# Loading k and v of batch 0 over SyncE's queue as 32-bit words in a fused attention and gated feed-forward kernel

## The chip, the cores and the metric

The kernel runs on one core of one Trainium2 chip. The metric is device time in microseconds, the median of the runs. The core has five engines with a queue each, worked through in order: TensorE (PE in the profile; PEld is its weight load), VectorE (DVE), ScalarE (ACT), GpSimd (POOL) and SyncE (SP). SyncE and GpSimd issue DMAs, which 16 DMA engines carry out. SBUF is the working memory with 128 partitions, PSUM the memory that TensorE writes.

## The reference

Eight batches of attention with keys and values averaged over groups of 8 rows, followed by a gated convolution feed-forward layer. Inputs and the output are 32-bit floats.

```python
# q, k, v: (8 batches, 8 heads, 576 rows, 64)
k_p = k.reshape(B, H, 72, 8, D).mean(axis=3)
v_p = v.reshape(B, H, 72, 8, D).mean(axis=3)
scores = (1/sqrt(D)) * q @ k_p.T
attn = softmax(scores)
x = (attn @ v_p), heads side by side            # (8, 576, 512)
h = maximum(x @ w_in, 0)                        # (8, 576, 1024)
c = sum over 3 taps of conv_w[tap] * h shifted by tap - 1 rows
out = (h * sigmoid(c)) @ w_out                  # (8, 576, 512)
```

## The kernel before

All arithmetic but the sums in PSUM is on 16-bit floats (bf16). Inputs are 32-bit in memory; GpSimd's DMAs convert them while they load (`nc.gpsimd.dma_start`), so every load of q, k, v and the weights stands in GpSimd's queue. SyncE's queue holds the convolution weights' load (L566), the stores of the output (L1106, L1116), and for batches 5 to 7 transposing DMAs (qT at L777, xT at L881).

Each batch goes through the same steps. **Loads**: `load_k` (L493 for 512 rows, L497 for the last 64), `load_v` (L526 main part, L533 and L538 for the tail), `load_q` (L456, L450). k_b, v_b and q_b have two buffers each, batch b uses number b % 2. **k**: VectorE adds 8 neighbours in three steps (L683, L691, L704), TensorE transposes the sums (L717, L718), and two copies spread them into kz (L724). **q**: a regrouping copy q<-q_b (L464, batches 0 to 4), transposes on TensorE (L794), copies to qT (L803). **v**: the same pooling (L683, L691, L754) and two masked products into vblk (L764, L759). **Attention**: scores on TensorE (L826, L828), exp on ScalarE (L834), five row tiles of attention times v (L851, L855; called av), division by the sum on VectorE (rr L864, xx L868), and the transpose of xx to xT (TensorE L891, L889 with copies L897; a DMA from batch 5 on). **Feed-forward**: x times w_in (L911 for batch 0, L934 for the others), the clipped result hT (L918, L940), convolution either as products on VectorE and ScalarE (cv: L982, L980, L989, L999) or on TensorE (L1057), the gate tg on ScalarE (L1007, L1064), its rescaling where the gate is a tanh (L1035), the product gT (L1045), and for each pair of batches the output projection with w_out (L1088), its copy to osb (L1111, L1101) and the store.

The order of all instructions is made when the program is built. `Planner.add` records every step with its engine, an assumed cost, what it reads and writes, and a priority; `Planner.order` then takes the steps one after the other by the earliest start that its costs give and, among equals, by the number in `PARAMS["prio"]`. Steps that may run on ScalarE or VectorE run on ScalarE if `PARAMS["act"]` names them. The program is emitted in that order, and each engine's queue keeps it; semaphores are added only where data, a buffer or one of the eight semaphore lanes of a DMA queue demand it. The planned order is all that carries over: an assumed cost is no wait. Where the planner finds TensorE waiting in the first 60 us, it emits filler matmuls on a tile of zeros (L418, from `warm`), which stand in TensorE's queue like any other instruction.

Before the change, GpSimd's queue starts with: the last 8 rows of q of batch 0 (L456), k of batch 0 (L493, L497), the identity matrix, one tail of v, the first 64 rows of q (L456), then the two halves of v (L526) with the other tails (L533) and the mask's instructions (L617, L621) between them, k of batch 1, and w_in. The staging tiles that the change uses are parts of gT, which batch 0 and 1 fill only from 30 us on:

```python
def early(i, lo, hi):
    return gT[i].rearrange("p f s -> p (f s)")[:, lo:hi].bitcast(FP32)
ks = early(1, 0, NT * 1024).rearrange("p (t e) -> p t e", t=NT)
ws = early(0, 0, NT * 1024).rearrange("p (t e) -> p t e", t=NT)
```

Of the kernel before, what the change touches and what calls it, by code (L numbers as in the profile page):

```python
# [14 lines left out]

PARAMS = {
    "prio": (
        "9 18 2 13 23 17 24 21 48 19 31 16 33 27 53 30 41 43 47 59 61 10 44 40 34 39 28 25 "
        "37 71 38 36 29 62 32 46 22 15 3 11 6 54 8 12 5 1 64 7 0 26 42 14 35 49 45 20 "
        "4 78 81 51 55 91 95 173 209 50 57 60 63 58 56 66 52 82 83 98 101 65 74 75 80 88 72 73 "  # L20
        "89 76 92 110 93 94 84 87 69 79 77 68 70 90 108 99 102 105 111 114 122 97 129 113 117 86 96 100 "
        "106 109 104 115 120 125 130 116 119 123 132 131 103 67 112 121 144 127 137 133 139 147 179 172 182 187 189 203 "
        "186 193 107 190 197 207 218 213 192 200 216 219 210 215 221 222 194 224 229 261 238 242 248 232 240 246 251 255 "
        "236 228 241 250 253 243 244 247 257 279 245 252 256 263 267 118 124 148 151 142 145 161 166 178 176 167 171 162 "
        "181 184 196 198 135 136 140 143 128 134 138 141 153 152 159 160 146 149 157 165 168 183 175 169 170 180 156 174 "
        "163 188 201 205 204 211 214 225 150 155 154 158 164 202 185 85 177 208 195 235 227 271 277 284 287 295 312 331 "
        "329 342 345 346 357 355 371 374 191 126 233 199 206 212 217 220 226 231 230 234 254 223 260 270 237 239 262 265 "
        "276 283 269 282 264 258 327 333 325 339 274 266 353 358 368 365 377 383 391 375 367 381 379 394 376 378 384 414 "
        "417 397 402 401 437 446 413 416 422 439 444 272 281 285 290 321 317 286 298 291 299 302 324 338 307 316 296 304 "
        "343 348 320 310 335 334 336 356 361 289 303 301 314 337 341 311 306 315 319 322 349 352 280 288 268 273 308 293 "  # L30
        "305 278 330 318 350 354 359 363 386 393 387 403 410 429 463 449 454 464 500 512 515 249 259 292 275 294 300 313 "
        "370 372 382 362 373 396 407 389 405 399 392 297 326 332 328 366 360 427 441 415 420 436 440 411 419 425 431 450 "
        "451 455 471 474 461 468 434 530 535 487 504 501 534 541 489 483 502 508 518 494 511 509 537 542 481 490 503 510 "
        "496 523 514 536 528 533 552 546 568 572 478 495 516 524 525 529 498 548 538 549 554 562 600 611 531 540 467 472 "
        "621 628 475 479 484 485 497 638 639 539 551 521 527 555 560 581 545 570 563 595 598 647 650 656 666 592 609 698 "
        "683 694 696 710 715 309 323 344 340 347 351 380 388 395 400 412 409 424 426 418 423 421 438 459 574 582 430 565 "
        "390 398 404 432 406 466 469 442 448 452 457 473 476 480 488 547 544 532 571 578 585 590 593 602 608 588 594 597 "
        "612 618 596 603 607 620 625 601 610 616 587 624 553 566 550 558 567 604 619 586 627 631 652 645 657 651 606 613 "
        "564 573 617 583 630 589 644 659 671 653 699 700 579 584 614 626 605 623 637 629 633 648 660 663 686 690 556 576 "
        "575 580 661 655 640 641 670 679 691 681 695 705 720 736 741 689 721 734 756 768 750 773 766 783 802 369 364 428 "  # L40
        "408 443 433 435 447 453 458 658 692 677 664 684 513 591 561 445 519 456 462 465 505 493 729 733 711 726 707 714 "
        "727 735 731 739 747 757 767 777 764 769 771 791 780 786 788 793 784 781 796 804 787 799 795 808 632 636 615 634 "
        "675 669 673 662 687 693 706 704 723 728 643 649 635 642 682 708 665 742 722 748 754 759 770 790 646 688 654 674 "
        "701 697 703 719 730 737 738 746 755 761 667 678 672 680 716 713 743 724 744 758 765 763 749 782 792 732 801 809 "
        "816 812 822 842 850 854 460 482 557 543 477 470 486 492 506 507 718 709 668 725 702 491 385 499 526 599 517 520 "
        "522 622 685 762 775 800 797 776 779 774 785 745 751 806 813 798 814 815 818 819 824 817 820 827 832 849 847 925 "
        "857 831 858 856 867 825 828 823 821 837 829 839 834 843 845 860 851 855 871 875 877 866 865 886 878 888 874 889 "
        "897 900 907 915 917 852 853 859 862 864 869 881 872 873 880 879 890 893 899 833 835 895 892 861 884 848 882 894 "
        "904 921 913 923 927 933 943 946 941 952 950 965 966 955 962 985 996 997 559 569 577 778 789 794 753 752 740 760 "
        "772 676 712 717 807 803 830 836 810 838 840 844 805 811 841 846 863 868 826 870 901 905 909 912 914 920 922 928 "  # L50
        "940 931 937 939 930 936 945 949 885 887 876 883 934 911 938 898 953 959 964 960 973 976 916 926 924 951 919 956 "
        "957 961 947 980 983 978 992 993 908 918 891 906 929 932 948 942 935 944 958 954 968 967 902 910 896 903 972 971 "
        "975 969 986 984 1009 990 1010 1011 1013 1019 1026 1034 1030 1036 1046 1041 1047 1020 1001 1015 998 988 1027 991 1017 1007 1023 1025 "
        "1028 1029 1035 1039 1016 1021 970 977 1031 1040 987 1002 989 999 1008 1043 1044 979 994 995 1000 1022 1024 1003 1004 1006 1014 1012 "
        "1018 1033 974 981 963 982 1005 1037 1032 1038 1072 1042 1051 1045 1049 1048 1054 1056 1052 1050 1055 1057 1053 1058 1061 1066 1073 1059 "
        "1062 1065 1060 1063 1067 1069 1068 1064 1070 1071 "
    ),
    "off": [(0, 2, 3, 6, 7), (0, 3, 4, 6, 7), (0, 1, 2, 3, 5, 6, 7), (0, 1, 2, 3, 4, 5, 6, 7), (0, 1, 2, 3, 4, 5, 6, 7), (0, 1, 2, 3, 4, 5, 6, 7), (0, 1, 2, 3, 4, 5, 6, 7), (0, 1, 3, 5, 7)],
    "seq": "",
    "sw": [0, 1, 0, 0, 1, 0, 0, 1],  # L60
    "fuse": [0, 0, 0, 0],
    "act": (
        "dw1.0 dw1.1 dw2.0 dw2.1 dw2.2 dw4.0 dw4.1 dw5.0 dw5.1 dw5.2 dw6.0 dw6.2 "
        "kz.0.0 qg.0.0 qTe.0.3 xte.0.0 xte.0.1 xte.0.2 xte.0.3 xte.0.4 kz.1.0 kz.1.1 qTe.1.2 xte.1.0 "
        "xte.1.1 xte.1.2 xte.1.3 xte.1.4 cp2.0.3 cp0.0.7 cp2.0.6 oe.0.0 oe.0.1 oe.0.2 kz.2.0 kz.2.1 "
        "qg.2.0 qTe.2.2 xte.2.0 xte.2.3 cp2.1.0 cp0.1.3 cp2.1.3 cp0.1.7 oe.0.4 oe.0.5 oe.0.7 oe.0.8 "
        "kz.3.1 qg.3.0 qg.3.4 qTe.3.0 qTe.3.1 qTe.3.2 xte.3.1 xte.3.4 cp2.2.0 cp0.2.3 cp0.2.5 oe.1.0 "
        "oe.1.1 oe.1.2 kz.4.0 kz.4.1 qTe.4.0 qTe.4.1 qTe.4.2 xte.4.0 xte.4.1 xte.4.2 xte.4.4 cp2.3.1 "
        "cp0.3.2 cp2.3.2 cp0.3.4 cp2.3.6 oe.1.4 oe.1.6 oe.1.7 oe.1.8 cp0.4.2 cp0.4.3 cp2.4.4 oe.2.0 "
        "oe.2.1 oe.2.2 kz.6.0 kz.6.1 cp2.5.3 cp2.5.4 cp0.5.6 cp0.6.0 cp2.6.0 cp2.6.2 cp2.6.3 cp0.6.4 "  # L70
        "cp2.6.4 cp2.6.5 cp2.6.6 oe.3.0 oe.3.1 oe.3.2 cp0.7.0 cp2.7.1 cp2.7.5 oe.3.4 oe.3.5 oe.3.8.0 "
        "oe.3.8.1 "
    ),
    "shift": {},
    "tail": [291.3594, -207.6026, 217.4942, 142.1234, 247.0674],
# [27 lines left out]
    "xw": 1,  # L103
    "qd": [0, 0, 0, 0, 0, 0, 0, 0],
    "vp": [0, 0, 0, 0, 0, 0, 0, 0],
    "kh": 0,
    "sp": [0, 0, 0, 0],
}

# [8 lines left out]
class Planner:  # L118
# [60 lines left out]
    def order(self):  # L179
# [23 lines left out]
        while avail:  # L203
# [68 lines left out]
            if o.dma is not None:  # L272
                n, each = o.dma
                if e == "SP" and s < 20.0 and o.lat is not None:
                    o.done = s + d + 2.03
                elif e == "SP" and s < 20.0:
                    hring = max(hring, s + d + 0.5, 3.9, max(ring)) + n * each
                    ring = [max(z, hring) for z in ring]
                    o.done = hring + self.DMA_LAT
                elif e == "SP":  # L280
                    late = max(ring) > s + d + 1.0
                    hring = max(hring, s + d + (4.5 if late else 0.5)) + n * each + (1.4 if late else 0.0)
                    for z in range(4):
                        ring[z] += n * each + 0.2 if late else 0.0
                    o.done = hring + (self.DMA_LAT if o.lat is None else o.lat)
                else:
                    w = (3,) if o.width == 1 else range(o.width)
                    for z in w:
                        ring[z] = max(ring[z], s + d + self.DMA_GAP)
                        ring[z] += n * each * (1.2 if ring[z] < 12.0 else 1.0 if ring[z] < 28.0 else 1.08)  # L290
                    x = max(ring)
                    land = x + self.DMA_LAT + (0.0 if x < 28.0 else 1.0)
                    o.done = x + (self.DMA_LAT if o.lat is None else o.lat) + (0.0 if x < 28.0 else 1.0)
            else:
                o.done = s + d + (self.LAT[e] if o.lat is None else o.lat) + self.SEM
            if e == "POOL" and o.dma is not None:
# [21 lines left out]
def kernel(  # L318
# [77 lines left out]
    pl = Planner()  # L396
# [442 lines left out]
    def attn_av(b, t, pr):  # L839
# [39 lines left out]
        if PARAMS["tx"][b]:  # L879
            def fn(e):  # L880
                nc.sync.dma_start(out=xT[m][:, :, u0:u0 + n], in_=xx[i3][0:n, :], transpose=True)  # L881
            pl.add(f"xD.{b}.{t}", "SP", 1.35, fn, reads=[("xx", i3)], writes=[("xT", m, t)], prio=pr + 0.3, dma=(1, 0.65), lat=0.4)
            return

        def fn(e):
# [344 lines left out]
```

## Time and profile before

| what | us |
|---|---|
| median of 3 runs | 201.35 (200.82 to 201.89) |
| the profiled execution | 201.61 |
| its span, first to last instruction | 199.6 |
| TensorE busy | 190.4 |
| VectorE busy | 167.7 |
| ScalarE busy | 168.4 |
| GpSimd busy | 48.0 |
| bytes moved by DMA | 30.02 MB, 150 GB/s in the mean |

A line of the costliest groups reads: line of the code, engine, operation, out<-in, shapes and types, count, then busy us and mean ns of one, then the engine's idle time just before and what ended it. A line of the timeline reads: start, length, engine, line, operation, count, with idle time and its end in brackets. A line of the chain of waits reads: start, length, what held the chain. A line of DMA issues ends with the KB of one and the median us from issue to landing. Busy times contain the overlap of pipelined instructions, so they say little on how full an engine is. The granted clock of TensorE is 0.999.

### The profile page before, as it was taken

The numbers are of one execution on the slowest core, as the hardware profiler recorded it, in microseconds if no ns is written. First come the engines' busy times: TensorE is split into PE (matmuls) and PEld (weight loads), VectorE is DVE, ScalarE is ACT, GpSimd is POOL, SyncE is SP. The second block draws the span as 40 slices with busy tenths as digits, with TensorE's granted clock in tenths as the row PEclk, the third lists the DMA queues.
The fourth block names the chain that finished last, engine by engine and source line by source line (L and its number), as shares of the span: only waits on it lengthen the run. The fifth ranks groups of instructions, "written<-read, shape, count | busy, mean of one in ns | idle before, by whom it ended". The sixth has DMA issues, their size and how long they took to land.

```text
span 199.6 us, 4550 instructions
## 1 busy us (share of the span) xinstructions
PE 190.4 (95%) x1768; PEld 131.6 (66%) x1768; DVE 167.7 (84%) x391; ACT 168.4 (84%) x289; POOL 48.0 (24%) x76
## 2 busy tenths in 40 slices
PE   4999999999999999999999999998899999999992
PEld 3998778887655766688787544554577865666441
DVE  5558799999999978999999999994589999968510
ACT  0955899999999997999999999964599999998421
POOL 7958234144250454364410000000000000000000
PEclk9999999999999999999999999999999999999999
DMA  3999999999999999999994047669733033220344
GB/s 32 184 202 204 204 197 206 198 201 209 193 184 237 247 223 213 201 181 142 151 127 72 30 120 211 106 174 165 190 117 57 3 65 104 83 105 0 141 179 158
DMA packets 52858, 30.02 MB, mean 150 GB/s; under 512 B 33484, under 2 KB 48356, under 8 KB 52836
## 3 DMA queue, kind: packets, MB, share of 16 engines
q0 software_dynamic: 32912, 16.73, 63.5%
q1 hardware_dynamic: 19924, 12.99, 25.9%
q8 instruction: 14, 0.23, 0.4%
q14 instruction: 8, 0.07, 0.1%
HBM read 33.44 MB, written 9.44 MB: 215 GB/s over the span
## 4 chain that ended last, share of the span: by engine, by line
PE 38%; DMA 34%; ACT 18%; issue 2%; DVE 2%; POOL 1%; SPq 1%; ACTq 0%; DVEq 0%; POOLq 0%
PE psfB L1088 13%; PE psfA L934 12%; DMA q<-in_q_dram 10%; DMA k_b<-in_k_dram 10%; DMA v_b<-in_v_dram 7%; ACT tg L1007 5%; DMA q_b<-in_q_dram 4%; ACT attnT L834 3%; ACT hT L918 2%; PE psfA L851 2%; ACT cv L980 2%; DMA xT<-xx 2%; PE psfA L1088 2%; PE pswB L418 2%; PE psfA L826 2%
## 5 line engine op out<-in xcount | busy, mean ns | idle before, releaser
L1088 PE MATMUL psfB<-w_out,gT 128*128 128x512 bf16 x272 | 63.0, 379 | 0.1
L934 PE MATMUL psfA<-xT,w_in 128*128 128x288 bf16 x448 | 59.0, 286 | 1.6 <-DMA xT<-xx 1.6
L934 PEld LDWEIGHTS <-w_in 128*128 128x128 bf16 x448 | 42.8, 98 | 14.0 <-DMA xT<-xx 1.9
L1088 PEld LDWEIGHTS <-gT 128*128 128x128 bf16 x290 | 27.5, 98 | 30.3 <-issue 0.7
L940 ACT ACTIVATE hT<-psfA 128x576 bf16<-128x576 f32 x56 | 36.1, 663 | 4.3 <-PE psfA L934 4.0
L982 DVE TENSOR_SCALAR cv<-hT,cr 128x576 bf16<-128x576 bf16 x76 | 26.0, 367 | 5.1 <-ACT hT L940 3.3
L1007 ACT ACTIVATE tg<-cv,cn 128x576 bf16<-128x576 bf16 x38 | 29.0, 804 | 0.6 <-DVE cv L999 0.6
L868 DVE TENSOR_TENSOR xx<-psfA,rr 128x512 bf16<-128x512 f32 (+1 forms) x40 | 26.5, 676 | 1.0 <-DMA xT<-xx 0.8
L834 ACT ACTIVATE attnT<-psfA 128x576 bf16<-128x576 f32 x40 | 25.1, 680 | 0.1
L1045 DVE TENSOR_TENSOR gT<-tg,hT 128x1152 bf16<-128x1152 bf16 x32 | 23.7, 749 | 1.1 <-ACT tg L1007 1.1
L980 ACT ACTIVATE cv<-hT,cr 128x576 bf16<-128x576 bf16 x32 | 24.4, 799 | 0.1
L989 DVE TENSOR_TENSOR cv<-cv,hT 128x1152 bf16<-128x1152 bf16 (+1 forms) x31 | 20.7, 674 | 1.0 <-ACT cv L980 0.9
L999 DVE TENSOR_TENSOR cv<-cv 128x1152 bf16<-128x1152 bf16 (+1 forms) x31 | 20.8, 673 | 0.4 <-ACT cv L980 0.3
L1111 ACT COPY osb<-psfB 128x512 f32<-128x512 f32 x21 | 12.9, 613 | 8.0 <-PE psfB L1088 6.5
L418 PEld LDWEIGHTS <-zero 128*128 128x128 bf16 x237 | 15.9, 107 | 3.2 <-DVE zero L558 2.5
L851 PE MATMUL psfA<-vblk,attnT 128*128 128x130 bf16 x160 | 15.5, 221 | 0.5 <-ACT hT L940 0.3
L1111 DVE COPY osb<-psfB 128x512 f32<-128x512 f32 x13 | 8.8, 683 | 6.6 <-PE psfB L1088 6.6
L418 PE MATMUL pswA<-zero 128*128 128x128 bf16 x144 | 11.3, 248 | 2.5 <-DVE zero L558 2.5
L851 PEld LDWEIGHTS <-attnT 128*128 128x128 bf16 x160 | 11.4, 98 | 3.4 <-issue 1.0
L826 PE MATMUL psfA<-qT,kz 128*128 128x512 bf16 x64 | 12.3, 286 | 0.0
L1007 ACT ACTIVATE tg<-cv,cs 128x576 bf16<-128x576 bf16 x16 | 12.1, 817 | 0.0
L855 PE MATMUL psfA<-vblk,attnT 128*128 128x130 bf16 x80 | 11.2, 222 | 0.0
(97 smaller groups left out, 257.5 us busy)
## 6 DMA issues: line engine op xcount, KB each, us to landing
out_dram<-osb SPq DMA_DIRECT2D x14, 512.0 KB, 3.6
k_b<-in_k_dram POOLq DMA_DIRECT2D x8, 512.0 KB, 14.8
v_b<-in_v_dram POOLq DMA_DIRECT2D x7, 512.0 KB, 15.0
q_b<-in_q_dram POOLq DMA_DIRECT2D x4, 576.0 KB, 17.5
out_dram<-osb SPq DMA_DIRECT2D x7, 256.0 KB, 2.5
w_in<-in_moe_w_in_dram POOLq DMA_DIRECT2D x2, 512.0 KB, 8.6
w_out<-in_moe_w_out_dram POOLq DMA_DIRECT2D x2, 512.0 KB, 14.4
q<-in_q_dram POOLq DMA_DIRECT2D x8, 128.0 KB, 12.2
```

The source lines that it names most:

```text
L418: nc.tensor.matmul(out=t, lhsT=zero[:, 0:P], rhs=zero[:, 0:P], start=True, stop=True)
L834: nc.scalar.activation(out=attnT[m][:, t, :], in_=slot(key).rearrange("p i x -> p (i x)")[:, 0:S], func=ACT.Exp, scale=1.0 / 64.0)
L851: nc.tensor.matmul(out=a[:, g, c * w:(c + 2) * w], lhsT=attnF[m][:, s * S + u0:s * S + u0 + P], rhs=vblk[m][:, 2 * s:2 * s + 2, :].rearran ...
L868: nc.vector.tensor_tensor(out=xx[i3][0:n].rearrange("p (g h e) -> p g h e", g=2, h=4), in0=av_view()[:, :, :, 0:D], in1=rr[i3][0:n].rearra ...
L934: nc.tensor.matmul(out=t[:, i, 0:HC], lhsT=w_in[:, c, f * P:(f + 1) * P], rhs=xT[m][:, c, i * HC:(i + 1) * HC], start=(c == 0), stop=(c == ...
L940: nc.scalar.activation(out=h_(b)[:, f, hs(b), 2:S + 2].rearrange("p (i x) -> p i x", i=2), in_=slot(key)[:, :, 0:HC], func=ACT.Relu)
L980: nc.scalar.activation(out=cv[y][:, kk // 2, z0:z1, :], in_=src, func=ACT.Copy, scale=sc)
L982: nc.vector.tensor_scalar(out=cv[y][:, kk // 2, z0:z1, :], in0=src, scalar1=sc, scalar2=None, op0=OP.mult)
L1007: nc.scalar.activation(out=tg[i3][:, zs[z0]:zs[z0] + z1 - z0, :], in_=cv[y][:, 0, z0:z1, :], func=ACT.Tanh if half else ACT.Sigmoid, scale ...
L1045: nc.vector.tensor_tensor(out=o_, in0=tg[i3], in1=h2, op=OP.mult)
L1088: nc.tensor.matmul(out=a[:, 0, j0:j1], lhsT=g[:, c, t * P:(t + 1) * P], rhs=w_out[:, c, j0:j1], start=(c == 0), stop=(c == n_fb - 1), skip ...
L1111: copy_on(e)(out=osb[i3][:, x, :], in_=slot(key)[:, 0, :])
```

## The change

`PARAMS["kh"]` goes from 0 to 3. With that value the code takes branches that were there already, for batch 0 alone:

```python
# load_k: 32-bit words over SyncE, L478 and L482 in the new numbering
nc.sync.dma_start(out=ks[:, 0:4], in_=src[0:512].rearrange("(t p) e -> p t e", p=P))
nc.sync.dma_start(out=ks[0:64, 4], in_=src[512:576])
# load_v: gate0, a GpSimd copy that needs k's first part and writes into ws (L505)
nc.gpsimd.tensor_copy(out=ws[0:16, 0:5:2, 0:1], in_=ks[0:16, 0:3, 0:1])
for c in range(4):                                              # L509
    nc.sync.dma_start(out=ws[32 * c + 16:32 * c + 32, 4], in_=src[P:P + 16, c])
for x in range(2):                                              # L513
    nc.sync.dma_start(out=ws[:, 2 * x:2 * x + 2], in_=src[0:P, 2 * x:2 * x + 2])
# gate1, a GpSimd copy that needs q of batch 0 (L1141)
nc.gpsimd.tensor_copy(out=scr[0:72], in_=q_b[0][0:72, 0, 0, 0:1])
```

The first pooling step then reads ks or ws, 32-bit, instead of k_b or v_b; VectorE clears the parts of ks and ws that no load fills. The planner makes every load of GpSimd but q of batch 0 depend on gate1, so in GpSimd's queue they stand behind both gates. All queues get a new order and some steps another engine:

```diff
 PARAMS = {
     "prio": (
-        "9 18 2 13 23 17 24 21 48 19 31 16 33 27 53 30 41 43 47 59 61 10 44 40 34 39 28 25 "
...
+        "16 10 3 26 23 18 29 57 28 35 49 46 54 65 56 8 20 22 15 24 30 9 40 52 47 34 41 39 "
...
     "act": (
-        "dw1.0 dw1.1 dw2.0 dw2.1 dw2.2 dw4.0 dw4.1 dw5.0 dw5.1 dw5.2 dw6.0 dw6.2 "
-        "kz.0.0 qg.0.0 qTe.0.3 xte.0.0 xte.0.1 xte.0.2 xte.0.3 xte.0.4 kz.1.0 kz.1.1 qTe.1.2 xte.1.0 "
...
+        "dw1.0 dw1.1 dw1.2 dw2.0 dw4.0 dw4.1 kz.0.1 qTe.0.0 qTe.0.2 xte.0.0 xte.0.1 xte.0.3 "
+        "xte.0.4 kz.1.0 kz.1.1 qTe.1.0 qTe.1.1 xte.1.0 xte.1.1 xte.1.3 xte.1.4 cp0.0.0 oe.0.0 oe.0.2 "
...
-    "kh": 0,
+    "kh": 3,
@@ Planner.order
-                        ring[z] += n * each * (1.2 if ring[z] < 12.0 else 1.0 if ring[z] < 28.0 else 1.08)
+                        ring[z] += n * each * (1.2 if ring[z] < 12.0 else 1.0 if ring[z] < 28.0 else 1.03)
                     x = max(ring)
-                    land = x + self.DMA_LAT + (0.0 if x < 28.0 else 1.0)
-                    o.done = x + (self.DMA_LAT if o.lat is None else o.lat) + (0.0 if x < 28.0 else 1.0)
+                    land = x + self.DMA_LAT + (0.0 if x < 28.0 else 0.4)
+                    o.done = x + (self.DMA_LAT if o.lat is None else o.lat) + (0.0 if x < 28.0 else 0.4)
@@ attn_av
-            pl.add(f"xD.{b}.{t}", "SP", 1.35, fn, reads=[("xx", i3)], writes=[("xT", m, t)], prio=pr + 0.3, dma=(1, 0.65), lat=0.4)
+            pl.add(f"xD.{b}.{t}", "SP", 1.35, fn, reads=[("xx", i3)], writes=[("xT", m, t)], prio=pr + 0.3, dma=(1, 0.65), lat=0.7)
```

The last three edits change assumed costs of the planner, and so the order alone. Line numbers of the new kernel are one less than before's from L58 on. In the engines' queues the counts change as follows. ScalarE: the four copies q<-q_b go (VectorE has ten instead of six), 6 dw products and 3 kz copies go, 5 cv products, 2 osb copies and 2 table loads come. VectorE: besides these, 5 narrow rescalings of tg come and 2 wide ones go, 5 cv products go. TensorE: 214 filler pairs instead of 237, and the same real matmuls in another order. Ahead of the first q transpose its queue holds 10, 80 and 16 fillers (12, 83 and 33 before). SyncE: the eight loads come right behind the convolution weights; all but one of the transposing DMAs of q stand ahead of those of xT.

## The prediction

> **What bounds the kernel now.** I read the page first: the busy shares, then the costliest groups.
>
> ```profile
> PE 190.4 (95%) x1768; PEld 131.6 (66%) x1768; DVE 167.7 (84%) x391; ACT 168.4 (84%) x289; POOL 48.0 (24%) x76
> ...
> L1088 PE MATMUL psfB<-w_out,gT 128*128 128x512 bf16 x272 | 63.0, 379 | 0.1
> L934 PE MATMUL psfA<-xT,w_in 128*128 128x288 bf16 x448 | 59.0, 286 | 1.6 <-DMA xT<-xx 1.6
> ```
>
> A mean of 379 ns contains overlap. What an instruction costs its engine is the distance from its start to the next start where nothing waits, its pitch. The chain of waits and the timeline give it:
>
> ```profile
> 13.22 0.69 PE psbB L794 x16
> ...
> 149.39 6.86 PE psfA L934 x56
> ...
> 161.62 6.91 PE psfB L1088 x32
> ```
>
> So 0.122 us for a matmul of L934 and 0.216 for one of L1088. With the other pitches of the timeline (a tile of L851 and L855 0.35, of scores 0.25 to 0.37, of L1057 0.74), all real matmuls in TensorE's queue sum to 170.0 us. The timeline of PE then shows where the other 30 of 199.6 us go:
>
> ```profile
> 4.54 6.48 PE L418 MATMUL pswA<-zero 128*128 128x128 bf16 x83
> ...
> 11.14 2.01 PE L418 MATMUL pswA<-zero 128*128 128x128 bf16 x33
> 13.22 0.69 PE L794 MATMUL psbB<-ident,q 72*128 72x72 bf16 x16
> ```
> ```profile
> 44.24 8.00 PE L934 MATMUL psfA<-xT,w_in 128*128 128x288 bf16 x64
> ```
> ```profile
> 138.69 0.29 PE L934 MATMUL psfA<-xT,w_in 128*128 128x288 bf16 x1
> 140.59 2.01 PE L934 MATMUL psfA<-xT,w_in 128*128 128x288 bf16 x15 [1.61 <-DMA xT<-xx]
> ```
>
> Three stretches. Until 13.22 TensorE runs only fillers (L418, counted as busy) and a few transposes. From 13.22 to 44.24 it fills batch 0 and 1 in, with 6.8 us of fillers between. From 44.24, the first matmul of batch 1's input projection (call it T1), to 195.9 it has 147.0 us of work in 151.7: 4.7 lost, 1.8 of it in the stall at 138.69. So TensorE bounds the kernel after T1, and a change pays by moving T1 forward, by leaving less work behind it, or by cutting the 4.7. After TensorE's end 3.7 us stay.
>
> In the fill the limit is VectorE. Summing pitches (xx 0.60, a 128x1152 add 0.67, cv 0.29, k pooling 0.73), it has 18.6 us between the last xx of batch 0 (ends 22.9) and that of batch 1 (ends 43.1), 20.2 us. The waits name the rest:
>
> ```profile
> DVE cv L982 <- ACT hT L918: 1.5, 1, 1.5
> ```
>
> **Term 1, the start.** Today q of batch 0 comes last:
>
> ```profile
> 4.66 7.72 DMA q_b<-in_q_dram
> ```
>
> It is issued behind k and shares the stream with v's two halves; k lands by 8.2 (its pooling starts at 8.29) and q at 12.38. The change takes two k and six v DMAs from GpSimd's queue and puts eight on SP's. SP's price has no row for such a load; the nearest are its stores and the weights' load:
>
> ```profile
> out_dram<-osb SPq DMA_DIRECT2D x14, 512.0 KB, 3.6
> ...
> out_dram<-osb SPq DMA_DIRECT2D x7, 256.0 KB, 2.5
> ```
>
> 1.1 us per 256 KB, so 1 MB from an issue at 1.25 lands near 1.25 + 3.6 + 2.2 = 7.05; bounds 6.0 (data moving from 2.2 us at the later rate) and 8.2 (nothing gained). Before q's main part GpSimd now issues eleven memsets and selects, pitch 0.04 to 0.3: issue at 3.9 to 4.7, today 4.66. Its 512 KB need 2.6 us at the 200 GB/s of the page. It lands at 9.3 if alone, at 11.2 if k's end and v's start share the engines, at 12.4 if nothing is gained; I take 10.6. But TensorE's queue holds 80 fillers, five transposes and 16 fillers ahead of the first q transpose. Where 83 took 6.27, 80 take 6.1, from the same 4.54; with 0.35 for the transposes and 16 x 0.06 it is free at 11.95. Any q landing up to 11.2 (plus 0.75 for VectorE's copy) is hidden behind these fillers. Term: 11.95 - 13.22 = **-1.3**, bounds -1.3 and 0.
>
> Added waits: GpSimd's gate0 waits for k, gate1 for q; behind them stand w_in, q, k and v of batch 1. SP's two large v loads wait for gate0; nothing else of SP is due until the first store. v is needed only when the exps of batch 0 end (today v's tiles are done at 17.74, exps at 17.8): issued near 8, its 1.2 MB land by 13, 2 us of cover; 32-bit pooling costs two instructions of at most 1.0 us by xx's row (512 elements of 32 bits in 0.60) where 0.42 and 0.55 stand. For k the same row bounds 1280 elements by 1.5 against 0.83; it ends near 9.5, under the fillers. The memsets of the staging tiles fall into VectorE's first 4 us.
>
> The Trainium skill, "VectorE: DVE Perf Modes" (walkthrough of the modes), says a 32-bit tensor_tensor stays at one result a cycle of 0.96 GHz; by that k's pooling would take 1.33 us, an estimate, and the sum is the same. No row of before shows it.
>
> **Term 2, the fill.** In the new VectorE queue the two q copies of batch 1 and its k pooling (2 x 0.62 + 0.73 = 2.0 us) stand between batch 0's last xx and the first cv, which covers the 1.5 us wait above; work between the two marks stays 18.6. Against it: v of batch 1 is pooled 7.1 us of VectorE work after that mark, about 28.5, and lands in my reckoning between 28.3 and 29.5 (today, 2 to 3 loads later in the queue, by 30.5). -1.5 and +0.7 give **-0.8**, bounds -1.5 and +0.7. ScalarE has 3.0 us less in this stretch (23.5 to 20.5: its q copies of 1.90 go to VectorE, where one takes 0.62) and can't hold it.
>
> **Term 3, work left behind T1.** Two score tiles (0.25 each) and one k transpose set (0.3) that stand ahead of T1 now stand behind it: **+0.8**, certain from the queues.
>
> **Term 4, after T1.** (a) The 138.69 stall: from the last attention tile of batch 5 to its first L934 there are 5.3 us of TensorE work now and 6.1 in the new order; gone it is worth -1.8. (b) New tight places: batch 2's first L934 stands 1.8 us of work after its last attention tile, today 8.4. VectorE must do 27.7 us from batch 1's last xx to batch 2's, TensorE only 26.5 from T1 to there (today 26.8 against 33.3); with 1.2 us for the transpose and its copy TensorE waits about 2. (c) Batch 5: VectorE 84.9 us of work after batch 1's xx, 4.2 idle as it has today over that stretch (43.1 to 134.6 for 87.2), and 3.6 to land xT, against 86.8 + 2 for TensorE: another 2 us. Two extra table loads (1.3 each) lie on ScalarE, whose sum falls by 6 us. Losses become 2 + 2 + 0.7 = 4.7 against 4.7: **0**, bounds -2.9 (neither stall) and +3.5 (VectorE idles 8 us).
>
> Sum: -1.3 - 0.8 + 0.8 + 0 = **-1.3**. The profiled execution took 201.61 for a span of 199.6; it becomes 200.3 and 198.3. The median is 0.26 lower: 201.35 - 1.3 = 200.05, say **200.0**.
>
> **Rivals.**
>
> *The queues share one stream.* Between 5 and 12.5 us the loads of before already move at 173 to 200 GB/s (the table of windows), as fast as later. If v's words, released at k's landing, delay q to 12.4, term 1 is 0 and the sum is 0: **201.3**. For it: v's halves and q overlap today too. Against: 1.2 us of slack under the fillers. The Trainium skill, "DMA: Bandwidth & Descriptors" (Issuing engines are not separate DMA queues), speaks for this rival: DMAs of all issuers run on the same 16 engines and interleave, so another issuer saves only issue time. The trace agrees that a shared stream costs q time: 7.72 us from issue to landing, against 2.6 us for its bytes alone.
>
> *VectorE becomes the bound after T1* (slower). It has 91.7 us of work from batch 1's last xx to batch 4's last gT, TensorE 92.0 from T1 to the output projection that needs it (today 84.3 against 84.7, with 4.2 idle taken from TensorE's own losses). If it idles as it does in today's fill, 1.6 in 20.2 us, that is 7.3 instead of 4.2: -1.3 + 3.1 = +1.8, **203.2**. It decides once VectorE idles more than 1.3 us beyond today's 4.2. For it: the tighter places of (b) and (c), and 3 us more VectorE work. Against: its loads come no later.
>
> *Neither stall comes.* Then losses fall by 2.9: **197.2**.
>
> **How the numbers follow.** Forecast 0.45, with 198.6 to 200.8 of its own; shared stream 0.2; VectorE 0.25; no stalls 0.1. The bounds of the terms add to -4.9 and +5.0, which need every end at once; the range 197.0 to 204.0 takes in all four cases. This kernel's measurement tells about 0.5% (1.0 us) from no change. Faster: 0.38 of the forecast's, 0.1, and 0.03 of the shared stream, 0.51. Same: 0.07 + 0.12, 0.19. Slower: 0.25 + 0.05, 0.30.
>
> **What would show it.** First q transpose at 11.95 with VectorE's copy done before it (term 1); T1 at 42.1 and no 1.5 us wait of VectorE for the first hT (term 2); waits of L933 (L934's new number) of about 2 us at batch 2 and at batch 5, total loss after T1 4 to 5 us (term 4). Wrong would be: q landing after 11.2; v of batch 1 after 29.5; a T1 later than 43; a TensorE that loses more than 7 us after T1, with VectorE never idle.

## The result, and the profile after

The changed kernel takes 207.91 us (median of four executions, 206.07 to 208.64) where the kernel before took 201.43 in the same session: ratio 1.031, 95% interval 1.024 to 1.038. Measured again later beside other kernels it was 1.0175 (1.010 to 1.025). Forecast were 200.0, in a range of 197.0 to 204.0. It is slower: the forecast was wrong in sign, and both measurements (medians 207.91 and 206.19) lie outside its range. The profiled execution took 208.64 us for a span of 206.9 (before 201.61 and 199.6). A ratio leaves out executions that lie more than 1.5% above the fastest of the same kernel, so it is not always the quotient of the medians.

The page of the changed kernel: shares of the engines, then the two costliest groups (numbers are one less than before's from L58 on).

```profile
PE 192.9 (93%) x1745; PEld 131.3 (63%) x1745; DVE 172.4 (83%) x403; ACT 166.7 (81%) x284; POOL 43.6 (21%) x70
...
L1087 PE MATMUL psfB<-w_out,gT 128*128 128x512 bf16 (+1 forms) x282 | 67.2, 384 | 0.5 <-ACT osb L1110 0.4
L933 PE MATMUL psfA<-xT,w_in 128*128 128x288 bf16 x448 | 59.7, 286 | 0.1
```

TensorE has the same real matmuls, and its input projection no longer waits (0.1 us idle ahead of L933 where 1.6 stood): the stall for xT at 138.69 is gone. Yet the span is 7.3 us longer. The timeline of PE shows where:

```profile
13.59 0.43 PE L793 MATMUL psbB<-ident,q 72*128 72x72 bf16 x8
...
26.62 0.53 PE L793 MATMUL psbB<-ident,q 72*128 72x72 bf16 x11 [1.35 <-DVE q L463]
...
46.58 7.02 PE L933 MATMUL psfA<-xT,w_in 128*128 128x288 bf16 x56
53.44 1.89 PE L1087 MATMUL psfB<-w_out,gT 128*128 128x512 bf16 x8
...
59.50 0.40 PE L716 MATMUL psbA<-ident,ksum 128*128 128x128 bf16 x4 [2.17 <-DVE ksum L703]
59.73 0.22 PE L717 MATMUL psbA<-ident,ksum 128*128 128x128 bf16 x1
60.37 3.44 PE L1087 MATMUL psfB<-w_out,gT 128*128 128x512 bf16 x8 [0.42 <-ACT osb L1110]
```

T1 is at 46.58, 2.3 us later than before and 4.5 later than forecast. From T1 to TensorE's end (203.27) are 156.7 us for 147.8 of work (the prediction's 147.0 and its 0.8): 8.9 lost, where 4.7 were lost before and forecast again. 4.5 + 4.2 make up the miss of 8.6 us of span (206.9 against 198.3). Most of the loss after T1 lies before 80 us.

The loads are behind both. GpSimd's timeline shows its two gates:

```profile
7.92 0.18 POOL L505 COPY gT<-gT 16x3 f32<-16x3 f32 x1 [3.51 <-DMA gT<-in_k_dram]
12.87 0.71 POOL L1141 COPY scr<-q_b 72x1 bf16<-72x1 bf16 x1 [4.77 <-DMA q_b<-in_q_dram]
13.52 1.14 POOL L545 DMA_DIRECT2D w_in<-in_moe_w_in_dram  x1
```

Behind gate1 (L1141) stand all loads of w_in and of batch 1. By the time the first of them is issued, at 13.52, q of batch 0 is in (12.75), v nearly (13.87), and nothing else is under way. The table of windows gives the start and end of a stretch and its length, then the busy time of PE, PEld, DVE, ACT and POOL, then the granted clock, the DMA share and GB/s. Two windows before the change:

```profile
13.00:15.00 2.00, 1.93 (x45) 1.67 (x43) 1.25 (x4) 2.00 (x3) 1.93 (x3) 1.00 1.24 203
15.00:17.00 2.00, 2.00 (x32) 1.15 (x29) 1.91 (x5) 1.92 (x4) 1.51 (x3) 1.00 1.23 202
```

The changed kernel:

```profile
11.00:13.00 2.00, 1.31 (x24) 1.14 (x22) 1.54 (x8) 0.00 (x0) 0.13 (x1) 1.00 1.07 273
13.00:15.00 2.00, 1.96 (x46) 1.67 (x44) 2.00 (x5) 1.07 (x3) 2.00 (x3) 1.00 0.61 221
15.00:17.00 2.00, 2.00 (x31) 1.21 (x28) 1.97 (x5) 1.93 (x4) 2.00 (x4) 1.00 0.86 91
```

The DMA share falls to 0.61 and 0.86: (1.24 - 0.61) / 1.24 x 2 + (1.23 - 0.86) / 1.23 x 2 = 1.6 us of the stream are lost. (The 221 GB/s beside 0.61 are no sign of the contrary: v comes as 32-bit words now, twice the bytes of the converted loads for the same elements.) VectorE then waits for q and k of batch 1 (the first two lines) and, 30 us later, for k of batch 3:

```profile
25.06 1.50 DVE L463 COPY q<-q_b 72x2048 bf16<-72x2048 bf16 x2 [1.81 <-DMA q_b<-in_q_dram]
27.85 0.82 DVE L682 TENSOR_TENSOR p<-k_b 128x1280 bf16<-128x1280 bf16 x1 [1.29 <-DMA k_b<-in_k_dram]
...
55.47 0.83 DVE L682 TENSOR_TENSOR p<-k_b 128x1280 bf16<-128x1280 bf16 x1 [2.87 <-DMA k_b<-in_k_dram]
```

The last 64 rows of k of batch 3 are the longest piece but one in the chain of waits:

```profile
3.71 9.05 DMA q_b<-in_q_dram
...
19.91 20.17 DMA v_b<-in_v_dram
...
40.36 15.09 DMA k_b<-in_k_dram
...
60.37 3.44 PE psfB L1087 x8
```

The last line is a second loss at the same place: eight matmuls of L1087 take 3.44 us where 1.89 is usual (the line at 53.44). The windows there:

```profile
57.00:59.00 2.00, 0.33 (x3) 0.02 (x1) 2.00 (x6) 0.59 (x1) 0.88 (x2) 1.00 1.24 202
59.00:61.00 2.00, 1.08 (x7) 0.58 (x8) 2.00 (x6) 2.00 (x5) 0.00 (x0) 0.89 1.38 189
61.00:63.00 2.00, 2.00 (x6) 0.76 (x5) 1.97 (x5) 0.68 (x2) 0.91 (x1) 0.50 1.40 186
63.00:65.00 2.00, 2.00 (x11) 1.09 (x10) 1.21 (x3) 1.06 (x2) 0.00 (x0) 0.76 1.27 192
```

TensorE idles from 57.2 to 60.4 but for five transposes, and behind that its granted clock is 0.50. Before the change it was 1.00 in the windows from 57 to 63 us.

### The profile page after: what moved, and what is told of

It reads as the page before. It is cut to its first block, busy times and chain, and to the rows that moved or that the text cites. A ratio compares the mean times of both kernels' runs of the same rounds, so it can differ in the third digit from the quotient of the medians.

```text
span 206.9 us, 4524 instructions
## 1 busy us (share of the span) xinstructions
PE 192.9 (93%) x1745; PEld 131.3 (63%) x1745; DVE 172.4 (83%) x403; ACT 166.7 (81%) x284; POOL 43.6 (21%) x70
## 4 chain that ended last, share of the span: by engine, by line
PE 54%; DMA 21%; ACT 9%; DVE 8%; POOL 4%; issue 2%; POOLq 0%
PE psfB L1087 25%; PE psfA L933 19%; DMA v_b<-in_v_dram 10%; DMA k_b<-in_k_dram 7%; DMA q_b<-in_q_dram 4%; PE psfA L850 2%; ACT attnT L833 2%; PE psfA L1056 2%; DVE cv L981 2%; ACT tg L1006 2%; PE psfA L825 2%; ACT osb L1110 1%; DVE p L682 1%; ACT qT L802 1%; PE psfA L854 1%
## 5 line engine op out<-in xcount | busy, mean ns | idle before, releaser
L1087 PE MATMUL psfB<-w_out,gT 128*128 128x512 bf16 (+1 forms) x282 | 67.2, 384 | 0.5 <-ACT osb L1110 0.4
L933 PE MATMUL psfA<-xT,w_in 128*128 128x288 bf16 x448 | 59.7, 286 | 0.1
L933 PEld LDWEIGHTS <-w_in 128*128 128x128 bf16 x448 | 42.8, 98 | 12.9 <-issue 0.4
L1087 PEld LDWEIGHTS <-gT 128*128 128x128 bf16 x290 | 28.1, 99 | 30.3 <-issue 2.8
L939 ACT ACTIVATE hT<-psfA 128x576 bf16<-128x576 f32 x56 | 35.4, 653 | 3.8 <-PE psfA L933 3.8
L1006 ACT ACTIVATE tg<-cv,cn 128x576 bf16<-128x576 bf16 x34 | 25.4, 783 | 4.2 <-DVE cv L998 2.6
L979 ACT ACTIVATE cv<-hT,cr 128x576 bf16<-128x576 bf16 x37 | 28.3, 787 | 0.3
L981 DVE TENSOR_SCALAR cv<-hT,cr 128x576 bf16<-128x576 bf16 x71 | 25.0, 373 | 4.0 <-ACT hT L939 3.7
L417 PEld LDWEIGHTS <-zero 128*128 128x128 bf16 x214 | 14.9, 111 | 4.0 <-DVE zero L557 3.2
L417 PE MATMUL pswA<-zero 128*128 128x128 bf16 x157 | 12.8, 251 | 3.2 <-DVE zero L557 3.2
L1006 ACT ACTIVATE tg<-cv,cs 128x576 bf16<-128x576 bf16 x20 | 14.9, 784 | 0.4 <-DVE cv L998 0.4
L1110 DVE COPY osb<-psfB 128x512 f32<-128x512 f32 x11 | 7.5, 686 | 5.7 <-PE psfB L1087 5.6
L854 PE MATMUL psfA<-vblk,attnT 128*128 128x130 bf16 x80 | 11.2, 221 | 0.0
```

The costliest lines, as they stand in the source:

```text
L417: nc.tensor.matmul(out=t, lhsT=zero[:, 0:P], rhs=zero[:, 0:P], start=True, stop=True)
L933: nc.tensor.matmul(out=t[:, i, 0:HC], lhsT=w_in[:, c, f * P:(f + 1) * P], rhs=xT[m][:, c, i * HC:(i + 1) * HC], start=(c == 0), stop=(c == ...
L939: nc.scalar.activation(out=h_(b)[:, f, hs(b), 2:S + 2].rearrange("p (i x) -> p i x", i=2), in_=slot(key)[:, :, 0:HC], func=ACT.Relu)
L979: nc.scalar.activation(out=cv[y][:, kk // 2, z0:z1, :], in_=src, func=ACT.Copy, scale=sc)
L981: nc.vector.tensor_scalar(out=cv[y][:, kk // 2, z0:z1, :], in0=src, scalar1=sc, scalar2=None, op0=OP.mult)
L1006: nc.scalar.activation(out=tg[i3][:, zs[z0]:zs[z0] + z1 - z0, :], in_=cv[y][:, 0, z0:z1, :], func=ACT.Tanh if half else ACT.Sigmoid, scale ...
```

## The experiments

**Theory A**: gate1 lets the DMA engines run empty, all loads come late, and the order by itself costs nothing. **Theory B**: the new order costs, above all because the last 64 rows of k of batch 3 stand behind w_out. **Theory C** (the rival of the prediction): VectorE is the bound after T1. Except where a diff shows otherwise, an edit is made where the planned order is emitted, so that all else keeps its place. The diffs give an edit in short; names like ldk3.t (the load of the last 64 rows of k of batch 3) are the planner's. All ratios are to the kernel before, measured in the same session.

**e1, new order, old loads.**

```diff
-  load_k, load_v of batch 0: nc.sync into ks, ws; gate0; gate1
+  load_k, load_v of batch 0: nc.gpsimd into k_b, v_b; no gates
```

> The new order of all queues, but k and v of batch 0 loaded over GpSimd with conversion into bf16, as before the change, and no gates. Theory A (the gates let the DMA engines run empty near 14 us, every later load comes 3 us late, and the order costs nothing by itself): about the time before, 201.4 +- 1, with T1 (the first matmul of batch 1's input projection) near 44 and v of batch 1 landing by 30. Theory B (the new order itself is what costs: batch 1's q and k are wanted early and batch 3's last 64 rows of k stand behind w_out in GpSimd's queue): 206 to 208, the idle stretch of TensorE near 57 us stays.

Ratio 1.0096 (1.004 to 1.015), from four of ten executions; in the other six, 205.24 to 206.35 us, the clock fell to 0.991 or 0.992, and with them the median is 205.33, 1.8% above the 201.73 of before. T1 stands at 44.05, as theory A has it, and from there to TensorE's end are 152.8 us, 5.0 lost (in the profiled execution, the fastest of the ten). So the loading accounts for the lost T1, and theory A is wrong in the rest: 1% or more stays with the order.

**e2, old order, new loads with both gates**, and **e10, the same without gate1.**

```diff
-  ldk0, ldv0: nc.gpsimd into k_b, v_b
+  ldk0, ldv0: nc.sync into ks, ws; gate0 (e2: and gate1) ahead of ldk1 in GpSimd's queue
```

> The old order of all queues, with k and v of batch 0 over SyncE as 32-bit words, gate0 and gate1 in GpSimd's queue ahead of its loads of k of batch 1. Theory A: the late loads cost here as well, 203.5 to 206, batch 1's v landing near 33. Theory B: 200.5 to 202, since the old order has slack for them.

> The old order of all queues with k and v of batch 0 over SyncE as 32-bit words and gate0 alone (e2 without gate1). If gate1 is what made e2 slower than before: T1 back at 44 to 44.5, ratio 0.996 to 1.003. If the 32-bit loads themselves cost (q of batch 0 late, v late): T1 at 45 or later, ratio 1.005 to 1.01.

e2: 1.0099 (1.0065 to 1.0134), T1 at 46.44. e10: 1.0000 (0.997 to 1.003), T1 at 44.63. So gate1 costs 1.0%, 2 us, in the old order too, and the 32-bit loads with gate0 are worth nothing and cost nothing within 0.3%. Window 13 to 15 of e2, then of e10:

```profile
13.00:15.00 2.00, 0.53 (x10) 0.35 (x7) 1.36 (x3) 0.92 (x1) 2.00 (x6) 1.00 0.70 111
```
```profile
13.00:15.00 2.00, 2.00 (x49) 1.88 (x46) 1.32 (x4) 1.66 (x3) 1.99 (x3) 1.00 1.19 245
```

**e3, no gates**, and **e7, gate0 only.**

```diff
-            o.fn(e)
+            if o.name not in ("gate0", "gate1"):    # e7: ("gate1",)
+                o.fn(e)
```

> The changed kernel without gate0 and gate1: w_in and the loads of batch 1 go out from 5 us on, and v of batch 0 right behind k. Theory A: the stream has no hole near 14 us, batch 1's k and v land 3 us earlier than in the changed kernel, T1 near 44, and the time is 203 to 204.5. Theory B: q of batch 0 lands later (14 or more) and takes the gain back, or the loads come early and nothing waits less behind T1: 206.5 to 208.5.

> The changed kernel without gate1, gate0 kept: w_in and the loads of batch 1 go out from 8 us on, behind k of batch 0 but beside its v and q. If the hole in the stream at 14 to 15.7 us is gate1's and makes the loads late: no hole, q of batch 1 lands by 23.5 instead of 25.0, T1 near 45, ratio to before 1.010 to 1.018. If the late T1 comes from q of batch 0 (12.8) sharing the stream with v: q lands at 14 or later, T1 stays at 46.5, ratio 1.02 to 1.03.

e7: 1.0146 (1.011 to 1.0185); no hole (DMA share 1.20 at 13 to 15), q of batch 1 is copied at 22.89, T1 at 43.98, as theory A says. What is left is the stop at k of batch 3 (1.91 us) and a clock of 0.50 behind it. e3: 1.0102 (1.006 to 1.014). Its stream has no hole either, but q of batch 0, now in company, is copied at 13.25 only; TensorE has used up its fillers, idles, and runs at half clock just there (windows 13 to 17 of e3):

```profile
13.00:15.00 2.00, 1.00 (x17) 1.01 (x18) 1.75 (x4) 0.40 (x1) 0.00 (x0) 0.63 1.12 262
15.00:17.00 2.00, 2.00 (x25) 1.56 (x23) 1.56 (x4) 1.34 (x3) 0.86 (x1) 0.50 1.25 202
```

so its T1 of 47.6, where theory A had 44, says nothing on the loads.

**e4, k's tail first**; **e8, the same without gates**; **e9, the same with gate0 only.**

```diff
+  ldk3.t emitted ahead of ldwo1 (GpSimd), three loads earlier
```

> The changed kernel with one DMA moved: the load of the last 64 rows of k of batch 3 stands ahead of w_out in GpSimd's queue instead of three loads later. Theory B: TensorE's idle stretch near 57 us (2.6 + 1.5 us) goes, and with it the fall of the granted clock to 0.50 behind it (1.7 us): 203 to 204.5. Theory A: the stretch gets shorter by at most 1 us because the main part of k of batch 3 and the q of batch 2 are late too: 206.5 to 207.9.

> The changed kernel without both gates and with the last 64 rows of k of batch 3 loaded ahead of w_out. If late loads are the main cause (gates early, the k tail later): about the new order with the old loads, ratio to before 1.005 to 1.012, no stop of TensorE over 1 us between T1 and 80. If the new order's VectorE work is what remains, still 3 to 5 us of loss after T1, in pieces under 1 us.

> The changed kernel without gate1 and with the last 64 rows of k of batch 3 loaded ahead of w_out, both corrections at once. If gate1 (2.6 us of T1) and the late k tail (3 to 4 us behind T1, with the fall of the clock) are the whole loss against before: T1 near 44, 152.5 us from T1 to TensorE's end, 201.5 to 202.8, ratio to before 0.997 to 1.005. If there is a third cause of the same size: ratio above 1.01.

e4: 1.0128 (1.005 to 1.021); its median of 203.94 lies where theory B put it, but the interval is too wide to tell it from the changed kernel's second measurement. The stop at k of batch 3 is gone; in its profiled execution, the slowest of four, some 3 us are lost between 60 and 70 instead, with q_b, v_b and w_out in the chain. e8: 1.0148 (1.009 to 1.021), above the 1.005 to 1.012 expected; no stop over 1 us behind T1 and 152.4 us from there, but it loses at the start as e3 does. e9: 1.0050 (1.001 to 1.009), at the upper end of its expectation, T1 at 43.90, 152.9 us behind it. e7 against e9 prices the late tail, with the clock, at 1.0%, 1.9 us; their intervals don't touch. In e9 TensorE passes the place without a wait:

```profile
54.51 0.39 PE L716 MATMUL psbA<-ident,ksum 128*128 128x128 bf16 x4
...
55.15 1.89 PE L1087 MATMUL psfB<-w_out,gT 128*128 128x512 bf16 x8 [0.20 <-ACT osb L1110]
```

**e13, the hole filled, gate1 kept**, and **e14, the changed kernel again.**

```diff
+  ldwi0 (half of w_in) emitted ahead of gate1
```

> The changed kernel with one load moved: the first half of w_in (1 MB in memory) goes out ahead of gate1, right behind gate0; all other loads of GpSimd still wait for q of batch 0. If it is the empty DMA engines at 14 to 16 us that cost, and not the wait as such: the hole is filled, q of batch 1 lands by 23.5 and T1 stands at 44 to 44.7, about as without gate1 (e7, ratio 1.0146): 1.010 to 1.020. If what counts is that q and k of batch 1 are issued late: T1 stays at 45 to 46.6 and the ratio at 1.02 to 1.03.

> The changed kernel itself, beside the others on the same chip. If gate1 and the late k tail are the whole loss: as first measured, ratio 1.024 to 1.038, of which e9 (ratio 1.005) took back all but 1 us. If its first four executions lay high by chance, with q of batch 0 at 12.8 in the profiled one: ratio 1.015 to 1.02, and q of batch 0 landing near 11.5.

e13: 1.0066 (1.003 to 1.0105), better than expected. e14: 1.0175 (1.010 to 1.025), its lower expectation: the first four executions lay high. GpSimd's timeline of e13 and its window:

```profile
7.87 0.79 POOL L545 DMA_DIRECT2D w_in<-in_moe_w_in_dram  x1 [0.27 <-issue]
11.70 0.70 POOL L1141 COPY scr<-q_b 72x1 bf16<-72x1 bf16 x1 [3.04 <-DMA q_b<-in_q_dram]
12.34 1.21 POOL L455 DMA_DIRECT2D q_b<-in_q_dram  x1
```
```profile
13.00:15.00 2.00, 2.00 (x47) 1.76 (x43) 2.00 (x5) 1.60 (x3) 2.00 (x4) 1.00 1.19 252
```

q of batch 1 is still issued only behind gate1, at 12.34, but the engines have w_in to move meanwhile. That issue is 1.0 us earlier than in e14 (13.37), where w_in stands ahead of it; yet in e7 and e9, which issue it at 8.68 and 8.33, its copy starts no earlier (22.89 and 22.86, against 22.63 in e13). So it is the empty stream that costs, not the wait and not the late issue. The intervals of e13 and e14 touch at their ends; the profiles carry this reading.

**e12, v held for q** (one execution).

```diff
-  gate0: copies from ks (k)
+  gate0: copies from q_b (q)
```

> The changed kernel with gate0 waiting for q of batch 0 instead of k, so that v of batch 0 goes out only when q is there. If v's words delay q: q lands at 9.5 to 10.5 instead of 11.5 to 12.8, the first q transpose stands at 11.95 (the fillers' end) and v, now late, holds the first attention tile until 18.5 or later. If q is bound by its own conversion or by k: q still lands at 11.5 or later.

209.32 us. q now lands at 11.21, 7.5 us from its issue, between the two expectations. With v's two large loads beside it, it lands at 11.3 to 11.7 in all other traces with gate0 but one. That one is the changed kernel's first profile: 12.75, with k's tail late too (9.39, in e12 8.46). So v's words cost q 0.1 to 0.5 us. Most of its time q spends behind k: from 5 to 8 us GpSimd's queue moves 0.17 MB beside k, from 8 to 10 it moves 0.40. The hole is deeper (DMA share 0.16, 0.00, 0.00 from 10 to 13).

The table has the kernels with the new order and SyncE's loads, but for e3 and e8, where the clock falls at the start. e4, e5 and e14 have both gates, e7, e9 and e11 gate0 alone (e5 and e11 come below).

| kernel | GB/s moved from 9 to 19 us | DMA share 13 to 15 | copy of q of batch 1 starts | T1 |
|---|---|---|---|---|
| e13, e11, e9, e7 | 241 to 244 | 1.17 to 1.20 | 22.51 to 22.89 | 43.35 to 44.17 |
| e14 | 211 | 0.69 | 24.03 | 45.27 |
| e4 | 208 | 0.35 | 24.31 | 45.66 |
| e5 | 201 | 0.34 | 24.16 | 45.16 |
| changed, first | 194 | 0.61 | 25.06 | 46.58 |
| e12 | 169 | 0.76 (0.00 from 11 to 13) | 26.73 | 47.74 |

The share of one window depends on where the hole lies in it; the bytes from 9 to 19 us take in all of it. e14 moves 0.30 MB less there than e13, 1.5 us of a stream of 200 GB/s. T1 follows the copy almost one for one, 20.8 to 21.5 us behind it.

**e5, fillers in the gap.**

```diff
             t = slot(key, True)
+            for i in range(38 if b == 3 else 0):
+                nc.tensor.transpose(out=t[:, 0, 0:P], in_=zero[:, 0:P], identity=ident)
```

> The changed kernel with 38 filler transposes of a tile of zeros (2.2 us by the fillers' pitch of 0.058) ahead of batch 3's k transposes, where TensorE stood idle from 56.9 to 59.4. If the idle time itself makes the granted clock fall to 0.50 behind it: clock 0.998 or more in most executions, L1087's eight matmuls behind it take 1.73 us again, 206.0 to 206.6. If the clock falls for another reason: 0.991 stays and so does 207.9.

206.18, ratio 1.0203 (1.017 to 1.0235). The clock is 0.997 to 1.000 in all four executions. Of the changed kernel's eight, five have 0.991 or 0.992, and they are its five slowest (206.97 to 208.64; the others 204.07 to 206.07). Its PE timeline:

```profile
55.75 2.29 PE L716 MATMUL psbA<-ident,zero 128*128 128x128 bf16 x38
57.93 0.40 PE L718 MATMUL psbA<-ident,ksum 128*128 128x128 bf16 x4
...
58.80 1.89 PE L1089 MATMUL psfB<-w_out,gT 128*128 128x512 bf16 x8 [0.42 <-ACT osb L1112]
```

The k transposes are as late as in e14 (57.98), and the eight matmuls behind them take 1.89, as usual. In the kernels without the stop, e4 and e9, none of 14 executions has a clock below 0.997; in e7, which has the stop and no fillers, three of four have 0.991 or 0.992. So the idle time lets the clock fall.

**e6, q copies back on ScalarE** (on e1) and **e11, thin q copies** (on e9).

```diff
-  o.fn(e)
+  o.fn("ACT" if o.name in ("qg.2.0", "qg.3.0", "qg.3.4") else e)      # e6
-  q2[...][0:PR, :, h:h + 4, :] from q_b[...]
+  q2[...][0:PR, :, h:h + 4, 0:4] for batches 2 and 3                   # e11
```

> The new order with the old loads (as e1), and the three copies q<-q_b of batches 2 and 3 that the change moved to VectorE back on ScalarE: 1.9 us less VectorE work between T1 and 75 us. If VectorE is what holds TensorE up after T1 in the new order: the loss after T1 falls from 5 to about 3 us and the time by 1.5 to 2 from e1's (ratio to before 1.000 to 1.004). If the loss hangs on the order or on the loads: within 0.5 us of e1.

> As e9, and the regrouping copies of q of batches 2 and 3 on VectorE copy 4 of 64 columns (the rest of that q is left over from batches 0 and 1): about 2 us less VectorE work between 40 and 75 us and nothing more on any other engine. If VectorE is the bound between T1 and 80 us: 1.5 to 2.2 us less than e9. If the loss there hangs on single waits: within 0.5 us of e9.

e6: 1.033 (1.0275 to 1.0385), far outside. It doesn't test what it was made for: the copies take 1.88 to 1.95 us each on ScalarE and hold up what stands behind them there:

```profile
59.43 1.89 PE L1087 MATMUL psfB<-w_out,gT 128*128 128x512 bf16 x8 [2.21 <-ACT osb L1110]
```

e11 takes 2.0 us from VectorE (two pairs of copies of 1.28 become 0.30): 1.0002 (0.997 to 1.004) against e9's 1.0050. That is 0.7 us of median, between the two expectations, and the intervals overlap. So VectorE holds at most a part of the loss behind T1; how much stays open.

## Why the prediction was wrong, step by step

**Term 1's added waits: the step that failed.** It named what stands behind gate1 (w_in, q, k and v of batch 1) and gave it no price. It should have asked what the DMA engines do between q's landing and the next load: once v is in, nothing. The reckoning kept the stream of 200 GB/s without a gap and let v of batch 1 land at 28.3 to 29.5. It landed at 33.2 (31.9 in e14), and at 29.6 to 30.5 where there is no hole (e1, e7, e9, e13). Price, by the middles of the ratios: 1.1% (e13 against e14) and 1.0% (e10 against e2), some 2 us. The signs that the prediction named for being wrong all came: q after 11.2, v of batch 1 after 29.5, T1 after 43, over 7 us lost behind it; only VectorE was not without idle time.

**Term 1, q's landing.** 10.6 was forecast; q is copied from 11.56 on in e14 and from 12.85 on in the first profile. e12 shows 11.2 even without v's large loads; 9.3 "if alone" left out the time behind k. SP's load of k's main part took 6.5 us, against 5.8 in the estimate:

```profile
gT<-in_k_dram SPq DMA_DIRECT2D x1, 1024.0 KB, 6.5
```

but the 128 KB tail issued behind it took 7.6, so k was pooled at 8.4 to 9.5. First q transpose: 13.59 and, in e14, 12.64, against 11.95. The new issuer brought no more speed: from 11 to 13 us e14 moves nothing but v's 32-bit words, 0.74 MB of them, where GpSimd's loads before the change moved 0.41 MB of 16-bit words, so fewer elements in the same time. The Trainium skill ("DMA: Bandwidth & Descriptors", Issuing engines are not separate DMA queues) states that the DMAs of all issuers run on the same 16 engines; the trace agrees. Nor does an earlier start carry on. In e10 there is none (first q transpose at 13.29, T1 at 44.63); in e9 the transpose stands 0.5 us earlier than before (12.68), but the first L910 is 0.2 later (22.27 against 22.08, as L911).

**Term 2.** The 1.5 us wait for the first hT is gone, as forecast, but the copies and the pooling that were to cover it wait themselves, 1.81 and 1.29 us. Where the loads come in time (e1, e7, e9), the way from the first L910 to T1 is 21.6 to 21.9 us against 22.16, so -0.3 to -0.5 where -0.8 was said; by the prediction's own marks, from the last xx of batch 0 to that of batch 1, it is 20.3 to 20.4 against 20.2, and nothing is gained.

**Term 3** (+0.8) holds as work: by the pitches of before, the matmuls behind T1 sum to 0.8 us more in the changed kernel's first trace. As time it was not measured by itself. e9 corrects both faults and still lies 1.0 us, 0.5%, above before; that is of its size, but it is the sum of all terms there.

**Term 4.** (a) The stall at batch 5 went. (b), (c): the two feared waits of 2 us at batch 2's and batch 5's first L933 never came. In e1, e8 and e9 4.6 to 5.1 us are lost behind T1, the 4.7 of the sum, by another way: pieces under 1 us between 50 and 80. In the changed kernel there comes on top what no term had: k of batch 3. Its tail was moved behind w_out in the queue and pushed back once more by the hole (issued at 24.79 and landed at 39.92 in the old order; issued at 40.36 in the changed kernel, 39.02 in e14, 36.85 in e13). That costs 1.9 us with the clock (e7 against e9). In e13, which keeps the late place, the tail lands 1.1 us earlier than in e7, the stop shrinks from 1.91 to 0.60 us and the clock stays up in eight of ten executions: a narrow margin.

**The rivals.** "VectorE becomes the bound" had the right sign, but mostly for another reason: half of the miss lies ahead of T1, and behind it TensorE stops for a late load. The argument against it, "its loads come no later", was the false one. e11 gives its mechanism 0.7 us by the middle values, not told apart from none. The shared stream was real, but v's words cost q only 0.1 to 0.5 us.

What stays open is the size of the two causes apart in the changed kernel itself. Its two measurements differ by more than one of them is worth, and the fall of the clock, which some executions have and some don't, is part of both. By other pairs gate1 costs 0.8% (e4, e9) and 0.3% or 1.6% (e7 against e14 or the first measurement), the late tail 0.5% or 1.8% (e4 against the same two). The prices can't be added either: 1.1, 1.0 and e9's 0.5 would make 2.6%, above e14's 1.75%, for filling the hole also brings the tail earlier.

## What to carry to other kernels

A wait put in front of a queue of loads is priced by what the DMA engines have left to move while it lasts: if the queue behind the gate holds the only bytes, every later load is late by what was not moved, and here a load with little slack showed it 40 us later. When an order changes, follow each load from its issue to its first reader, the small tails too. None of the corrected versions here beats the kernel before (the best, e10, equals it).

## What the runs showed of the hardware

The stop of TensorE ahead of L1087 costs 1.5 us more on the eight matmuls behind it (3.44 against 1.89): the granted clock falls to 0.50 for 3.4 us. A mean clock of 0.991 or 0.992 is what such a fall leaves, and five of eight executions of the same program have it; in e14's profiled execution the same stop passed without it. The clock records of the traces point to why. The changes of the clock lie whole multiples of 3.41 us apart, on a grid that stands elsewhere in each execution. The stretch of this grid that ends where the clock falls holds 2.6 us without a matmul in the changed kernel (57.13 to 60.54), and 1.8 to 2.3 in the other four such falls (e3, e7, e8, e12). In e14 a mark at 57.0 cuts the stop into two stretches with 1.0 and 1.4. No stretch behind which the clock stayed up holds more than 1.8. So the stop did not have to fill the stretch; about half of it was enough.

The Trainium skill ("TensorE: Matmul & The Clock Gate", Part 1) states a halved clock after an idle window of about 3.4 us that runs freely of the program. The 0.50, the length and the free grid agree with it; the stretches here were not idle throughout.

A 32-bit pooling instruction of 128x1280 took 1.49 us, as the prediction's bound of 1.5 had it, where the 16-bit one takes 0.83.
